# Part of w2 taken from the last load and brought in early by GpSimd, in a decode block on one Trainium2 core

## The chip, the cores and the metric

One core of a Trainium2 chip runs the whole program. The metric is the device time of one execution in microseconds; lower is better. The kernel before takes 1057.88 us (median of three runs, 1057.36 to 1058.01).

## What is computed

One token goes through a transformer block with conditioned layer norms. All arrays are fp32.

```
mod = (silu(c) @ w_mod).reshape(1, 6, 1, 640)      # sa, ca, ga, sb, cb, gb
h   = layernorm(x) * (1 + ca) + sa
x   = x + ga * attention(h, k_cache, v_cache, wq, wo)   # 32 heads, 8192 positions, 192 wide
h   = layernorm(x) * (1 + cb) + sb
x   = x + gb * (relu(h @ w1 + b1) ** 2 @ w2 + b2)       # 640 -> 1536 -> 640
```

The two caches are 403 MB together, each byte is used once, and all of it has to come from HBM.

## The kernel before

**Attention.** The loop over the 32 heads (L285) loads for each head the keys (`load_k`, one tile of 128 partitions by 64 positions by 192) and the values (`load_v`). A K tile carries, behind its keys, a slice of wq or wo that is needed soon. K, V and the large weights go round in three slots of one pool (`slot`, L54), so a load can be issued only when the tile that had its slot three allocations earlier has been read to the end. All of these loads are issued from SyncE's queue (SP), in program order; the instruction that issues one waits there for its slot.

`keys` (L192) multiplies the keys by the query on VectorE (L201), folds 7 of 16 positions in half on GpSimd (L203) and reduces on VectorE (L204, L205), in two pieces for a head and in four for the last one. `softmax` (L216) finds the maximum through a matmul with the identity (L220, L222) and takes the exponential on ScalarE (L228). `values` (L233) does 48 matmuls of p with V. `project` and `attend` carry the result of a pair of heads through wo. The order of every engine's instructions is the order in which the program is written (`manual_schedule`).

**Small columns.** `wm0`, the first load, ends with columns of x, c, b1 and b2 (L73); L76 copies them out. `spread` (L85) turns such columns into rows by a copy that repeats each value 32 times (L88) and a 32x32 transpose (L90); L284 makes `bbt`, the biases b1 and b2, before the first head.

**The tail.** After head 31 SyncE issues the rest of `wm1`, w1 in two pieces, gb, and w2 in five (L312 to L319). w2 comes last, since it is used last. Partition 32g+r holds the rows r, 32+r, ... of group g, where each of the four groups g has a quarter (384) of the 1536 hidden values; so w2 is 12 blocks b of 128 x 640, cut as 6, 3, 1, 1, 1 (`W2_CUT`). The compute of the tail is: `project(15)`, `attend(15)`, the residual and the second layer norm (L329 to L338), h @ w1 into four groups of 32 PSUM partitions, each 384 wide (`ps_f`, L343), bias, relu and square (`f`, L346 to L348), a transpose (`fT`, L349), the gate `gb` (L351), some matmuls into an unused bank (`ps_warm`, L355), then h @ w2 (`ps_y`, L363), 48 matmuls in order of b, and two VectorE instructions (L366, L367) before the output is stored (L368). A fp32 matmul of the program stands twice in the trace, as two passes.

Of the kernel before, what the change touches and what calls it, by code (L numbers as in the profile page):

```python
# [8 lines left out]
F32 = mybir.dt.float32  # L9
# [4 lines left out]
P = 128  # L14
D = 640
H = 32
# [3 lines left out]
G = 4  # L20
DG = D // G
FG = FF // G
KB = DG // 32
FB = FG // 32
PW = 2 * DH
E = 8
ED = 64
# [9 lines left out]
WITHOUT_W = (1, H - 2)  # L37
WITH_W = tuple(h for h in range(H) if h not in WITHOUT_W)
W1_CUT = ((0, 3), (3, 2))
W2_CUT = ((0, 6), (6, 3), (9, 1), (10, 1), (11, 1))  # L40
WARM = 2
EPS = 1e-5


@with_exitstack
def block_kernel(ctx: ExitStack, tc: tile.TileContext, kw, ky, vc, wm0, wm1, w1, gb, w2, out):
    nc = tc.nc
    const = ctx.enter_context(tc.tile_pool(name="const", bufs=1))
    strm = ctx.enter_context(tc.tile_pool(name="strm", bufs=3))
    work = ctx.enter_context(tc.tile_pool(name="work", bufs=2))  # L50
# [3 lines left out]
    def slot(name):  # L54
        return strm.tile([P, SLOT], F32, tag="slot", name=name, bufs=3)
# [16 lines left out]
    wm0_t = slot("wm0_t")  # L72
    nc.sync.dma_start(wm0_t[:, :wm0.shape[1]], wm0)  # L73

    small = const.tile([P, 2 * KB + FB + KB], F32, name="small")
    nc.vector.tensor_copy(small, wm0_t[:, KB * 2 * D + WQ:wm0.shape[1]])  # L76
    x_c, c_c, bbc = small[:, :KB], small[:, KB:2 * KB], small[:, 2 * KB:]

    def columns(src, n, name, pool=const, **how):

        t = pool.tile([P, n // 32, 32], F32, name=name, **how)
        nc.vector.transpose(t.rearrange("p b r -> p (b r)"), src)
        return t

    def spread(src, n, name):  # L85

        t = work.tile([P, FB + KB, 32], F32, name=name + "_c", tag="spread", bufs=1)
        nc.vector.tensor_copy(t[:, :n], src[:, :, None].to_broadcast([P, n, 32]))  # L88
        r = const.tile([P, 32 * n], F32, name=name)
        nc.vector.transpose(r, t[:, :n].rearrange("p b r -> p (b r)"))  # L90
        return r
# [38 lines left out]
    mods = const.tile([P, 6, DG], F32, name="mods")  # L130
# [19 lines left out]
    def load(src, to, h, what):  # L150
        to[h] = slot(f"{what}{h}")
        n, w = CUTS.get((what, h), 1), src.shape[1]
        for c in range(n):
            a, b = c * HD // n, (c + 1) * HD // n if c + 1 < n else w
            nc.sync.dma_start(to[h][:, a:b], src[:, a:b])

    def load_k(h):

        load(kw[WITH_W.index(h)] if h in WITH_W else ky[WITHOUT_W.index(h)], k_t, h, "k")

    def load_v(h):
        load(vc[h], v_t, h, "v")
# [14 lines left out]
    def query(i, w):  # L177
        w = w.rearrange("p (b n) -> p b n", b=KB)
        ps = psum.tile([P, 512], F32, tag="q", name=f"ps_q{i}", bufs=2)
        for b in range(KB):  # L180
            nc.tensor.matmul(ps[:, :PW], hR[:, b], w[:, b], start=(b == 0), stop=(b == KB - 1))  # L181
        qb_t[i] = work.tile([P, PW], F32, name=f"qb{i}", tag="qb")
        nc.scalar.activation(qb_t[i], ps[:, :PW], AF.Copy, scale=DH ** -0.5)  # L183
# [27 lines left out]
    def inverse(i):  # L211
        r = work.tile([P, 2], F32, tag="r", name=f"r{i}")
        nc.vector.reciprocal(r, sum_t.pop(i))
        ri_t[i] = r
# [30 lines left out]
    def project(i):  # L245

        n = 32 * NV
        os_ = work.tile([P, 2, ED], F32, tag="os", name=f"os{i}")
        inverse(i)
        r2 = ri_t.pop(i)  # L250
        for a in range(2):
            h = 2 * i + a
            om = work.tile([P, ED, E], F32, tag="om", name=f"om{h}", bufs=1)
            nc.vector.scalar_tensor_tensor(om[:n], ps_t.pop(h)[:n].rearrange("p (d e) -> p d e", e=E), r2[:n, a:a + 1],  # L254
                                           mask[:n, None, :].to_broadcast([n, ED, E]), op0=ALU.mult, op1=ALU.mult)
            nc.vector.tensor_reduce(os_[:n, a], om[:n], axis=AX.X, op=ALU.add)  # L256
        os_t[i] = psum.tile([P, 512], F32, tag="sm", name=f"ps_oT{i}", bufs=2)
        nc.tensor.matmul(os_t[i][:, :n], os_[:n].rearrange("p a d -> p (a d)"), quad[:n], start=True, stop=True)

    def attend(i, w):  # L260
        oT = work.tile([P, 96], F32, tag="oT", name=f"oT{i}")
        nc.vector.tensor_copy(oT, os_t.pop(i)[:, :96])  # L262
        w = w.rearrange("p (j n) -> p j n", j=3)
        if i + 1 < NPAIR:
            for j in range(3):
                for g in range(2):
                    nc.tensor.matmul(att_a[32 * g:32 * (g + 1), :2 * DG], oT[:, 32 * j:32 * (j + 1)],  # L267
                                     w[:, j, 2 * DG * g:2 * DG * (g + 1)], start=(i == 0 and j == 0), stop=(i == NPAIR - 2 and j == 2))
            return
        for j in range(3):  # L270
            for g in range(G):
                nc.tensor.matmul(att_t[0][32 * g:32 * (g + 1), :DG], oT[:, 32 * j:32 * (j + 1)],
                                 w[:, j, DG * g:DG * (g + 1)], start=False, stop=(j == 2))

    def gather():

        nc.scalar.activation(att_s[:64], att_a[:64, :2 * DG], AF.Copy)
        att_t.append(psum.tile([P, 512], F32, tag="o", name="att", bufs=3))
        for g in range(G):
            nc.tensor.matmul(att_t[0][32 * g:32 * (g + 1), :DG], ident[:, 32 * (g // 2):32 * (g // 2) + 1].to_broadcast([P, 32]),  # L280
                             att_s[:, DG * (g % 2):DG * (g % 2 + 1)], start=True, stop=False)

    x_t = spread(x_c, KB, "x_t")
    bbt = spread(bbc, FB + KB, "bbt")  # L284
    for h in range(H):  # L285
        i = h // 2
        if h:
            load_k(h)
        if h == H - 1:
            wm1_t = slot("wm1_t")  # L290
            nc.sync.dma_start(wm1_t[:, :WO + KB * D], wm1[:, :WO + KB * D])
        load_v(h)
        w = k_t[h][:, HD:]

        def between(c):
            if c == 0 and h % 2 and i:
                attend(i - 1, w)
            elif c == 0 and h % 2 == 0 and i + 1 < NPAIR:
                query(i + 1, w)
            elif c == 2 and h == H - 1:  # L300
                gather()

        if h % 2 and i:
            project(i - 1)
        sc = keys(h, between)
        p = softmax(h, sc)
        if h == H - 1:
            next(mod(2, 1, wm1_t[:, WO:WO + KB * D].rearrange("p (b n) -> p b n", b=KB)))
        values(h, p)
# [3 lines left out]
    w1_t = slot("w1_t")  # L313
# [3 lines left out]
    w2_t = slot("w2_t")  # L317
    for b0, n in W2_CUT:
        nc.sync.dma_start(w2_t[:, b0 * D:(b0 + n) * D], w2[:, b0 * D:(b0 + n) * D])  # L319
    gb_t = w1_t[:, KB * FF:KB * (FF + D)].rearrange("p (b n) -> p b n", b=KB)  # L320
    w1_t = w1_t[:, :KB * FF].rearrange("p (b n) -> p b n", b=KB)
    w2_t = w2_t[:, :FB * D].rearrange("p (b n) -> p b n", b=FB)

    project(NPAIR - 1)
    attend(NPAIR - 1, wm1_t[:, :WO])
    mod_b = mod(3, 2, wm1_t[:, WO + KB * D:WO + KB * 3 * D].rearrange("p (b n) -> p b n", b=KB), (2, 2, 1))
# [11 lines left out]
    hT2 = columns(layernorm(x1, 32, scale_b, lambda: mods[:, 3], "ln2", lambda: next(mod_b)), DG, "hT2")  # L338

    pf = psum.tile([P, 512], F32, tag="q", name="ps_f", bufs=2)  # L340
    for b in range(KB):
        for g in range(G):
            nc.tensor.matmul(pf[32 * g:32 * (g + 1), :FG], hT2[:, b], w1_t[:, b, FG * g:FG * (g + 1)],  # L343
                             start=(b == 0), stop=(b == KB - 1))
    f = work.tile([P, FG], F32, name="f", tag="spread", bufs=1)
    nc.vector.tensor_add(f, pf[:, :FG], bbt[:, :FG])  # L346
    nc.vector.tensor_scalar(f, f, 0.0, None, op0=ALU.max)
    nc.vector.tensor_mul(f, f, f)  # L348
    fT = columns(f, FG, "fT", work, tag="om", bufs=1)  # L349

    next(mod(5, 1, gb_t))  # L351
    idle = psum.tile([P, 512], F32, tag="sm", name="ps_warm", bufs=2)
# [1 line left out]
        for g in range(G):  # L354
            nc.tensor.matmul(idle[32 * g:32 * (g + 1)], ones[:, :32], w1_t[:, k, :512], start=True, stop=True)  # L355
    gb2 = const.tile([P, DG], F32, name="gb2")
    nc.vector.tensor_mul(gb2, mods[:, 5], bbt[:, FG:])
    nc.vector.tensor_add(x1, x1, gb2)

    py = psum.tile([P, 512], F32, tag="q", name="ps_y", bufs=2)  # L360
    for b in range(FB):
        for g in range(G):
            nc.tensor.matmul(py[32 * g:32 * (g + 1), :DG], fT[:, b], w2_t[:, b, DG * g:DG * (g + 1)],  # L363
                             start=(b == 0), stop=(b == FB - 1))
    y = const.tile([P, DG], F32, name="y")
    nc.vector.tensor_mul(y, py[:, :DG], mods[:, 5])  # L366
    nc.vector.tensor_add(y, y, x1)  # L367
# [43 lines left out]
```

## Time and profile before

| | |
|---|---|
| median of three runs | 1057.88 us |
| span of the profiled execution, from its first to its last instruction | 1055.5 us |
| busy in that span: TensorE, VectorE, GpSimd, ScalarE | 463.7, 831.4, 194.8, 33.4 us |
| read from HBM, mean rate | 451.82 MB, 428 GB/s |
| share of the 16 DMA engines that the load queue (q1) took | 99.3% |
| VectorE waiting for K tiles that carry a weight slice | 134.4 us |

The time of a run is 2.4 us more than the span of the profiled execution; what lies around the span isn't in the trace. The profile's page has one line for each engine's busy time, a picture of the span in 40 slices, the chain of work that ended last, and groups of instructions by line. The trace answers with waits (who waited for whom), with timelines of a stretch, and with busy times, granted TensorE clock and DMA share of a stretch. Line numbers (L201) are those of the kernel before.

### The profile page before, as it was taken

The page shows a single profiled execution, that of the slowest core. Times are in us where ns is not written, and L with a number is a line of the kernel's source. Part 1 is how long each engine was busy: PE and PEld are TensorE (multiplying, and loading weights), DVE is VectorE, ACT ScalarE, POOL GpSimd, SP SyncE. Part 2 cuts the span into 40 slices and gives each one's busy share as a digit, 9 for nine tenths or more (in the row PEclk, how much of TensorE's full clock was granted, in tenths as well). Part 3 has the DMA queues.
Part 4 walks back from the last instruction along what each step waited for, and adds up shares of the span by engine and source line. Part 5 has one row for each costly group of instructions (what it writes and reads, how often), then busy time and mean ns, then how long its engine had stood idle before and what let it go on. Part 6 is the DMA issues. An engine that isn't in the chain of part 4 may idle for free.

```text
span 1055.5 us, 5687 instructions
## 1 busy us (share of the span) xinstructions
PE 463.7 (44%) x2356; PEld 155.0 (15%) x2356; DVE 831.4 (79%) x409; ACT 33.4 (3%) x88; POOL 194.8 (18%) x72
## 2 busy tenths in 40 slices
PE   3234443355543345463334534335453335535446
PEld 1101111111111111120111111101111111111113
DVE  2886878978787987878888687997878798789963
ACT  1000000000000000000000000000000000000000
POOL 0211112211212221212221212221221221122110
PEclk9667666766666766666676666666666666767769
DMA  9999999999999999999999999999999999999997
GB/s 403 435 434 428 432 440 427 441 424 437 433 433 428 440 424 441 424 439 427 431 437 437 422 442 430 428 439 426 439 429 433 428 438 433 434 427 432 424 426 310
DMA packets 11410, 452.18 MB, mean 428 GB/s; under 512 B 1269, under 2 KB 1273, under 8 KB 1785
## 3 DMA queue, kind: packets, MB, share of 16 engines
q1 hardware_dynamic: 11384, 451.83, 99.3%
q8 instruction: 18, 0.29, 0.1%
q14 instruction: 8, 0.06, 0.0%
HBM read 451.82 MB, written 0.00 MB: 428 GB/s over the span
## 4 chain that ended last, share of the span: by engine, by line
DMA 42%; DVE 39%; PE 17%; ACT 1%; issue 1%; SPq 0%; DVEq 0%; ACTq 0%
DMA k<-in_kw 36%; DVE k L201 21%; PE ps_o L240 14%; DVE sc L204 12%; DVE sc L205 5%; DMA k<-in_ky 3%; DMA w_t<-in_w 2%; PE ps_mx L220 1%; DMA wm_t<-in_wm 1%; ACT p L228 1%; PE ps_sum L97 1%; PE ps_mod L140 1%; PE ps_q L181 1%; DVE nm L222 0%; DVE mp L218 0%
## 5 line engine op out<-in xcount | busy, mean ns | idle before, releaser
L201 DVE TENSOR_TENSOR k<-k,qb 128x6144 f32<-128x6144 f32 (+1 forms) x66 | 419.7, 6359 | 141.6 <-DMA k<-in_kw 134.4
L203 POOL TENSOR_TENSOR k<-k 128x1344 f32<-128x1344 f32 (+1 forms) x66 | 194.1, 2941 | 820.9 <-DVE k L201 476.1
L240 PE MATMUL ps_o<-v,p 128*32 128x512 f32 x1536 | 290.4, 731 | 17.2 <-ACT p L228 17.2
L204 DVE TENSOR_REDUCE sc<-k 128x18 f32<-128x3456 f32 (+1 forms) x66 | 240.5, 3644 | 4.3
L220 PE MATMUL ps_mx<-ident,mp 128*128 128x128 f32 x64 | 25.5, 501 | 416.2 <-DVE mp L218 416.2
L240 PEld LDWEIGHTS ps_o<-v,p 128*32 128x32 f32 x1536 | 68.4, 131 | 215.4 <-issue 193.1
L267 PE MATMUL att_a<-k,oT 128*32 128x320 f32 x180 | 49.6, 720 | 114.2 <-DVE oT L262 113.1
L205 DVE TENSOR_REDUCE sc<-k 128x14 f32<-128x1344 f32 (+1 forms) x66 | 99.0, 1500 | 0.0
L220 PEld LDWEIGHTS ps_mx<-ident,mp 128*128 128x128 f32 x64 | 16.1, 312 | 442.8 <-DVE mp L218 421.0
L181 PE MATMUL ps_q<-k,hR 128*128 128x384 f32 x150 | 52.3, 496 | 0.0
L228 ACT ACTIVATE p<-sc,nm 128x256 f32<-128x256 f32 x32 | 16.2, 508 | 760.6 <-DVE nm L222 496.9
L267 PEld LDWEIGHTS att_a<-k,oT 128*32 128x32 f32 x180 | 13.7, 161 | 136.7 <-DVE oT L262 116.7
L222 DVE TENSOR_REDUCE nm<-ps_mx 128x1 f32<-128x128 f32 x32 | 9.3, 291 | 28.5 <-PE ps_mx L220 28.5
L181 PEld LDWEIGHTS ps_q<-k,hR 128*128 128x128 f32 x150 | 27.3, 190 | 27.9 <-issue 11.7
L254 DVE SCALAR_TENSOR_TENSOR om<-ps_o,r,mask 96x512 f32<-96x512 f32 x32 | 23.9, 747 | 6.5 <-PE ps_o L240 5.4
L256 DVE TENSOR_REDUCE os<-om 96x64 f32<-96x512 f32 x32 | 21.8, 682 | 1.1
L140 PE MATMUL ps_mod<-wm_t,silu 128*32 128x320 f32 (+1 forms) x120 | 11.7, 550 | 14.6 <-DVE silu L128 14.6
L97 PE MATMUL ps_sum<-sp,ones 128*128 128x2 f32 x32 | 9.4, 364 | 17.2 <-ACT p L228 17.2
L183 ACT ACTIVATE qb<-ps_q 128x384 f32<-128x384 f32 x16 | 7.9, 491 | 195.2 <-PE ps_q L181 195.2
L97 PEld LDWEIGHTS ps_sum<-sp,ones 128*128 128x128 f32 x32 | 8.0, 312 | 21.9 <-ACT p L228 21.9
L145 DVE COPY mods<-ps_mod 128x320 f32<-128x320 f32 (+1 forms) x4 | 1.6, 398 | 10.2 <-PE ps_mod L140 10.2
L76 DVE COPY small<-wm_t 128x27 f32<-128x27 f32 x1 | 0.2, 179 | 11.2 <-DMA wm_t<-in_wm 11.2
(77 smaller groups left out, 90.9 us busy)
## 6 DMA issues: line engine op xcount, KB each, us to landing
k<-in_kw SPq DMA_DIRECT2D x29, 7104.0 KB, 27.4
v<-in_vc SPq DMA_DIRECT2D x32, 6144.0 KB, 22.1
k<-in_ky SPq DMA_DIRECT2D x1, 6144.0 KB, 28.3
k<-in_ky SPq DMA_DIRECT2D x2, 3072.0 KB, 21.5
k<-in_kw SPq DMA_DIRECT2D x3, 1536.0 KB, 15.5
wm_t<-in_wm SPq DMA_DIRECT2D x1, 4173.5 KB, 12.7
wm_t<-in_wm SPq DMA_DIRECT2D x1, 3200.0 KB, 29.3
wm_t<-in_wm SPq DMA_DIRECT2D x1, 2560.0 KB, 18.2
```

The lines of the kernel that those rows point to most:

```text
L97: nc.tensor.matmul(ps[:, :n], ones, src, start=True, stop=True)
L140: nc.tensor.matmul(ps[32 * g:32 * (g + 1), :n * DG], e[:, b:b + 1].to_broadcast([P, 32]), wb[:, :, DG * g:DG * (g + 1)], start=(b == 0), s ...
L181: nc.tensor.matmul(ps[:, :PW], hR[:, b], w[:, b], start=(b == 0), stop=(b == KB - 1))
L201: nc.vector.tensor_mul(pr, pr, q[:, None, :].to_broadcast([P, n, DH]))
L203: nc.gpsimd.tensor_add(half, half, pr[:, m:, DH // 2:])
L204: nc.vector.tensor_reduce(s[:, :m], pr[:, :m], axis=AX.X, op=ALU.add)
L205: nc.vector.tensor_reduce(s[:, m:], half, axis=AX.X, op=ALU.add)
L220: nc.tensor.matmul(ps[:, :P], mp.to_broadcast([P, P]), ident, start=True, stop=True)
L228: nc.scalar.activation(p, sc[:, :, None].to_broadcast([P, NPOS, 32 // E]), AF.Exp, bias=nm, accum_out=sp[:, h % 2:h % 2 + 1])
L240: nc.tensor.matmul(ps_t[h][32 * g:32 * (g + 1)], p[:, E * j:E * (j + 1)].rearrange("p e r -> p (e r)"), t[:, j, g], start=(j == 0), stop=( ...
L254: nc.vector.scalar_tensor_tensor(om[:n], ps_t.pop(h)[:n].rearrange("p (d e) -> p d e", e=E), r2[:n, a:a + 1], mask[:n, None, :].to_broadca ...
L267: nc.tensor.matmul(att_a[32 * g:32 * (g + 1), :2 * DG], oT[:, 32 * j:32 * (j + 1)], w[:, j, 2 * DG * g:2 * DG * (g + 1)], start=(i == 0 an ...
```

## The change

w2 is divided unevenly. The four groups now have 320, 320, 448 and 448 hidden values. The last load brings ten blocks for all 128 partitions (cut 5, 2, 1, 1, 1). Four more blocks, for partitions 64 to 127 alone, come from a new array `w2x` into a tile of their own, `w2x_t`. Behind them in each row of `w2x` stand 14 columns of b1 and 5 of b2, which leave `wm0`.

`w2x_t` is filled from GpSimd's queue in the iterations of heads 8, 10, ... 22. Each of these issues two transfers: the 19 bias columns (76 bytes a row) of eight rows of partitions 0 to 63, and eight rows of partitions 64 to 127 whole (2579 values, 10316 bytes a row). The eight rows are every fourth one of a group of 32. `bbt` is spread from `w2x_t`, 608 wide in place of 544, and this moves from before head 0 to the start of head 30's iteration, ahead of `keys(30)` on VectorE.

In the tail `ps_f` has groups 320 and 448 wide, `f` is 448 wide (a memset clears the part that partitions 0 to 63 don't have, and the bias is added in two instructions), and `ps_y` has 16 matmuls on partitions 64 to 127 with `w2x_t` ahead of 40 with w2.

```diff
-FB = FG // 32
+FB = 10
+FX = 4
+FT = FB + FX
+F0 = (0, 32 * FB, 64 * FB, 64 * FB + 32 * FT)
+FN = (32 * FB, 32 * FB, 32 * FT, 32 * FT)
+WX = FX * D + FT + KB
...
-W2_CUT = ((0, 6), (6, 3), (9, 1), (10, 1), (11, 1))
+W2_CUT = ((0, 5), (5, 2), (7, 1), (8, 1), (9, 1))
+X_AT = {8 + 2 * r: (r % 4) + 32 * (r // 4) for r in range(8)}
...
     x_t = spread(x_c, KB, "x_t")
-    bbt = spread(bbc, FB + KB, "bbt")
+    w2x_t = const.tile([P, WX], F32, name="w2x_t")
...
         load_v(h)
+        if h in X_AT:
+            r = X_AT[h]
+            top = 32 * (r // 32 + 1)
+            nc.gpsimd.dma_start(w2x_t[r:top:4, FX * D:], w2x[r:top:4, FX * D:])
+            nc.gpsimd.dma_start(w2x_t[64 + r:64 + top:4], w2x[64 + r:64 + top:4])
+        if h == H - 2:
+            bbt = spread(w2x_t[:, FX * D:], FT + KB, "bbt")
...
+    f = work.tile([P, 32 * FT], F32, name="f", tag="spread", bufs=1)
+    nc.vector.memset(f[:64, 32 * FB:], 0.0)
     project(NPAIR - 1)
...
-            nc.tensor.matmul(pf[32 * g:32 * (g + 1), :FG], hT2[:, b], w1_t[:, b, FG * g:FG * (g + 1)],
+            nc.tensor.matmul(pf[32 * g:32 * (g + 1), :FN[g]], hT2[:, b], w1_t[:, b, F0[g]:F0[g] + FN[g]],
                              start=(b == 0), stop=(b == KB - 1))
-    f = work.tile([P, FG], F32, name="f", tag="spread", bufs=1)
-    nc.vector.tensor_add(f, pf[:, :FG], bbt[:, :FG])
+    nc.vector.tensor_add(f[:, :32 * FB], pf[:, :32 * FB], bbt[:, :32 * FB])
+    nc.vector.tensor_add(f[64:, 32 * FB:], pf[64:, 32 * FB:32 * FT], bbt[64:, 32 * FB:32 * FT])
...
+    w2x_b = w2x_t[64:, :FX * D].rearrange("p (b n) -> p b n", b=FX)
+    for b in range(FX):
+        for g in range(G):
+            nc.tensor.matmul(py[32 * g:32 * (g + 1), :DG], fT[64:, FB + b], w2x_b[:, b, DG * g:DG * (g + 1)],
+                             start=(b == 0), stop=False)
     for b in range(FB):
         for g in range(G):
             nc.tensor.matmul(py[32 * g:32 * (g + 1), :DG], fT[:, b], w2_t[:, b, DG * g:DG * (g + 1)],
-                             start=(b == 0), stop=(b == FB - 1))
+                             start=False, stop=(b == FB - 1))
```

More of the change, by code (lines that the diff above doesn't have):

```diff
@@ L45, in block_kernel @@
 @with_exitstack
-def block_kernel(ctx: ExitStack, tc: tile.TileContext, kw, ky, vc, wm0, wm1, w1, gb, w2, out):
+def block_kernel(ctx: ExitStack, tc: tile.TileContext, kw, ky, vc, wm0, wm1, w1, gb, w2, w2x, out):
     nc = tc.nc
@@ L73, in block_kernel @@
     nc.sync.dma_start(wm0_t[:, :wm0.shape[1]], wm0)
-    small = const.tile([P, 2 * KB + FB + KB], F32, name="small")
+    small = const.tile([P, 2 * KB], F32, name="small")
     nc.vector.tensor_copy(small, wm0_t[:, KB * 2 * D + WQ:wm0.shape[1]])
-    x_c, c_c, bbc = small[:, :KB], small[:, KB:2 * KB], small[:, 2 * KB:]
+    x_c, c_c = small[:, :KB], small[:, KB:2 * KB]
     def columns(src, n, name, pool=const, **how):
@@ L85, in spread @@
     def spread(src, n, name):
-        t = work.tile([P, FB + KB, 32], F32, name=name + "_c", tag="spread", bufs=1)
+        t = work.tile([P, FT + KB, 32], F32, name=name + "_c", tag="spread", bufs=1)
         nc.vector.tensor_copy(t[:, :n], src[:, :, None].to_broadcast([P, n, 32]))
@@ L342, in block_kernel @@
         for g in range(G):
-            nc.tensor.matmul(pf[32 * g:32 * (g + 1), :FG], hT2[:, b], w1_t[:, b, FG * g:FG * (g + 1)],
+            nc.tensor.matmul(pf[32 * g:32 * (g + 1), :FN[g]], hT2[:, b], w1_t[:, b, F0[g]:F0[g] + FN[g]],
                              start=(b == 0), stop=(b == KB - 1))
-    f = work.tile([P, FG], F32, name="f", tag="spread", bufs=1)
-    nc.vector.tensor_add(f, pf[:, :FG], bbt[:, :FG])
+    nc.vector.tensor_add(f[:, :32 * FB], pf[:, :32 * FB], bbt[:, :32 * FB])
+    nc.vector.tensor_add(f[64:, 32 * FB:], pf[64:, 32 * FB:32 * FT], bbt[64:, 32 * FB:32 * FT])
     nc.vector.tensor_scalar(f, f, 0.0, None, op0=ALU.max)
     nc.vector.tensor_mul(f, f, f)
-    fT = columns(f, FG, "fT", work, tag="om", bufs=1)
+    fT = columns(f, 32 * FT, "fT", work, tag="om", bufs=1)
     next(mod(5, 1, gb_t))
@@ L356, in block_kernel @@
     gb2 = const.tile([P, DG], F32, name="gb2")
-    nc.vector.tensor_mul(gb2, mods[:, 5], bbt[:, FG:])
+    nc.vector.tensor_mul(gb2, mods[:, 5], bbt[:, 32 * FT:])
     nc.vector.tensor_add(x1, x1, gb2)
     py = psum.tile([P, 512], F32, tag="q", name="ps_y", bufs=2)
+    w2x_b = w2x_t[64:, :FX * D].rearrange("p (b n) -> p b n", b=FX)
[3 more added lines that the diff above has]
+                             start=(b == 0), stop=False)
     for b in range(FB):
@@ L385, in column, with hidden @@
         return a(v).reshape(G, n, 32).transpose(0, 2, 1).reshape(P, n)
+    def hidden(v):
+        b = np.zeros((P, FT), np.float32)
+        for g in range(G):
+            b[32 * g:32 * (g + 1), :FN[g] // 32] = a(v)[F0[g]:F0[g] + FN[g]].reshape(-1, 32).T
+        return b
+    w2 = a(B_w2)
+    w2m = np.stack([w2[F0[g]:F0[g] + 32 * FB].reshape(FB, 32, D).transpose(1, 0, 2) for g in range(G)])
+    w2e = np.stack([w2[F0[g] + 32 * FB:F0[g] + 32 * FT].reshape(FX, 32, D).transpose(1, 0, 2) for g in (2, 3)])
     wq = a(A_wq).reshape(G, KB, 32, NPAIR, PW).transpose(3, 0, 2, 1, 4).reshape(NPAIR, P, WQ)
@@ L396 @@
         "vc": a(A_v_cache).reshape(H, P, NPOS // E, E, NV, ED).transpose(0, 1, 2, 4, 5, 3).reshape(H, P, HD),
-        "wm0": np.concatenate([rows(wm[:, :2 * D], KB), wq[0], column(A_x, KB), column(c, KB),
-                               column(B_b1, FB), column(B_b2, KB)], axis=1),
+        "wm0": np.concatenate([rows(wm[:, :2 * D], KB), wq[0], column(A_x, KB), column(c, KB)], axis=1),
         "wm1": np.concatenate([wo[-1], rows(wm[:, 2 * D:3 * D], KB), rows(wm[:, 3 * D:5 * D], KB)], axis=1),
@@ L401 @@
         "gb": rows(wm[:, 5 * D:], KB),
-        "w2": rows(B_w2, FB),
+        "w2": np.ascontiguousarray(w2m.reshape(P, FB * D)),
+        "w2x": np.concatenate([np.concatenate([np.zeros((64, FX * D), np.float32), w2e.reshape(64, FX * D)]),
+                               hidden(B_b1), column(B_b2, KB)], axis=1),
     }
```

## The prediction, made before the change was run

> **What bounds the kernel now.** I read the page first (span, the DMA row, the chain), then the chain of waits over the last 150 us piece by piece, then VectorE's timeline there, and last the DMA share stretch by stretch. From the page, and from the view that divides the span into stretches (columns: length, busy time and count of each engine, granted TensorE clock, DMA share, GB/s):
>
> ```profile
> span 1055.5 us, 5687 instructions
> q1 hardware_dynamic: 11384, 451.83, 99.3%
> q8 instruction: 18, 0.29, 0.1%
> ```
> ```profile
> 31.00:939.00 908.00, 392.71 (x1784) 125.76 (x1785) 738.05 (x315) 26.57 (x75) 175.52 (x58) 0.68 1.00 433
> ```
>
> Until 939 us the 16 DMA engines are full, at 433 GB/s, which is 27.1 GB/s for each engine. In that stretch every byte added to the queue delays what is behind it. The question is what happens after 939. Two pieces of the chain that ended last (start, length, what):
>
> ```profile
> 912.48 26.83 DMA k<-in_kw
> 939.31 0.03 issue
> 939.34 0.02 DVEq L201
> 939.36 0.04 issue
> 939.40 6.57 DVE k L201
> ...
> 964.30 0.06 DVE nm L222
> 964.36 0.14 issue
> 964.50 6.56 DVE k L201
> ```
> ```profile
> 1032.07 19.60 DMA w_t<-in_w
> 1051.67 0.04 issue
> 1051.71 0.52 PE ps_y L363 x8
> ```
>
> and VectorE's timeline, where the bracket is the idle time before an instruction:
>
> ```profile
> 939.40 6.56 DVE L201 TENSOR_TENSOR k<-k,qb 128x6144 f32<-128x6144 f32 x1 [3.24 <-DMA k<-in_kw]
> 964.50 6.55 DVE L201 TENSOR_TENSOR k<-k,qb 128x6144 f32<-128x6144 f32 x1
> 999.05 0.26 DVE L262 COPY oT<-ps_oT 128x96 f32<-128x96 f32 x1 [0.38 <-PE ps_oT L258]
> 1030.28 0.74 DVE L254 SCALAR_TENSOR_TENSOR om<-ps_o,r,mask 96x512 f32<-96x512 f32 x1 [5.37 <-PE ps_o L240]
> ```
>
> Head 29's keys land at 939.31, and this is VectorE's last wait for a transfer. From there heads 29, 30 and 31 run one behind the other: VectorE, the maximum through TensorE, the exponential, 48 matmuls, `project`, the layer norm, `ps_f`, `f`, `ps_y`. No step of it before `ps_y` waits for data from HBM. So two strands meet at `ps_y`: a compute strand that hangs on 939.31, and the transfers of w2, which end at 1051.67. Today the transfers end last. How much later?
>
> ```profile
> 1044.38 1.57 PE L140 MATMUL ps_mod<-w_t,silu 128*32 128x160 f32 x40
> 1047.46 3.16 PE L363 MATMUL ps_y<-w_t,fT 128*32 128x160 f32 x80
> 1050.92 0.48 PE L363 MATMUL ps_y<-w_t,fT 128*32 128x160 f32 x8 [0.31 <-DMA w_t<-in_w]
> 1051.71 0.48 PE L363 MATMUL ps_y<-w_t,fT 128*32 128x160 f32 x8 [0.31 <-DMA w_t<-in_w]
> ```
>
> The gate's matmuls (L140) have the same shape and wait for nothing: 40 in 1.57, 0.039 us each. At that pace the 96 of `ps_y` would take 3.77 and end at 1051.2, where in the trace they end at 1052.2. So the compute strand has only **1.0 us of room**. That is the number to watch: anything over 1.0 us that is put on the compute strand lengthens the kernel.
>
> **The change, part by part.**
>
> *Fewer bytes at the end.* Two blocks less of w2 for all partitions: 2 x 128 x 2560 bytes = 655 KB, at 433 GB/s 1.5 us less on the last transfers. Worth at most 1.0 us, after which the compute strand ends last; and it is worth nothing if that strand grows.
>
> *The same bytes earlier.* Heads 8 to 22 lie in the stretch where DMA is full, so the 8 x 8 x 10316 = 660 KB delay all later tiles, head 29's keys among them. Spread over all 16 engines that is 660 KB / 433 = 1.5 us. But each transfer has eight rows. If eight engines take one row each and always the same eight, each of them gets 82.5 KB more, at 27.1 GB/s **3.05 us**, and a tile is complete when its slowest engine is. What matters then is whether those eight have room. At the end of the span the queue runs dry and shows this:
>
> ```profile
> 1047.00:1048.00 1.00, 1.00 (x25) 0.70 (x20) 0.67 (x3) 0.00 (x0) 0.00 (x0) 1.00 0.60 241
> 1048.00:1049.00 1.00, 1.00 (x39) 0.98 (x31) 0.00 (x0) 0.00 (x0) 0.00 (x0) 1.00 0.58 221
> 1049.00:1050.00 1.00, 0.98 (x31) 0.66 (x24) 0.00 (x0) 0.00 (x0) 0.00 (x0) 1.00 0.54 197
> 1050.00:1051.00 1.00, 0.69 (x24) 0.27 (x19) 0.00 (x0) 0.00 (x0) 0.00 (x0) 1.00 0.15 59
> ```
>
> A DMA share of 0.58 is nine engines of 16 at work: about seven are through shortly after 1047, nine only after 1049.5, and the last at 1051.67. So the engines do drift apart, by 3 to 4 us over the run. Seven are early, yet eight get the extra rows: whichever eight they are, at least one of the late nine is among them. That one ends 0 to 1.5 us ahead of the last, and so with 3.05 us more it ends 1.5 to 3.05 us after it. I take the middle: **head 29's keys 2.3 us late**. That the same engines are late by about as much at 939 as at the end is an estimate; the views don't name an engine. Below, 0 would be right if the drift had a different pattern there; above, a foreign packet on an engine may cost more than its bytes. The nearest row is q8, the instruction fetches: 0.1% of 16 x 1055.5 us over 18 packets is 0.94 us for 16 KB, where 27.1 GB/s gives 0.6; by that ratio 3.05 becomes 4.7 us, and that is the upper end.
>
> [...]
>
> *`bbt` spread at head 30.* The trace has both instructions, 544 wide:
>
> ```profile
> L88 DVE COPY bbt_c<-small x1: 720/720/720, 25.6 to 25.6; 128x544 f32<-128x544 f32 x1
> L90 DVE STREAM_TRANSPOSE bbt<-bbt_c x1: 746/746/746, 26.4 to 26.4; 128x544 f32<-128x544 f32 x1
> ```
> ```profile
> 31.56 6.56 DVE L201 TENSOR_TENSOR k<-k,qb 128x6144 f32<-128x6144 f32 x1 [4.44 <-ACT qb L183]
> ```
>
> Where they stood they cost nothing: VectorE idled 4.44 us behind them, until ScalarE delivered the first query, and that is gone with no gain. Their new place is 964.50, between two instructions with no gap: 1.466 x 608/544 = **1.64 us** on the compute strand. Queued behind them is everything from head 30 on, and SyncE's loads of head 31, w1 and w2 with it; these have enough transfers ahead of them to stay fed.
>
> *GpSimd.* Sixteen issues, each pair ahead of the fold of its head. GpSimd idles 16.5 us before such a fold (POOL L203 at 914.85, next fence), so some microseconds of issuing are hidden. If they took over 16, VectorE's L205 would be late. I cost them at nothing.
>
> ```profile
> 914.85 3.03 POOL L203 TENSOR_TENSOR k<-k 128x1344 f32<-128x1344 f32 x1 [16.48 <-DVE k L201]
> ```
>
> *The tail's compute.* From the groups of instructions by line (busy, mean ns) between 1039 and 1053:
>
> ```profile
> L343 PE MATMUL ps_f<-w_t,hT 128*32 128x384 f32 x40 | 5.1, 680 | 2.1 <-issue 2.1
> L355 PE MATMUL ps_warm<-w_t,ones 128*32 128x512 f32 x16 | 1.9, 592 | 0.0
> ```
>
> The four groups of a set run side by side. A set 512 wide takes 1.9/4 = 0.48 us, a set 160 wide 1.57/10 = 0.16, so 64 columns more are worth 0.06. If the widest group rules, ten sets of `ps_f` cost 0.6 us more; if the mean width rules, which stays 384, nothing; by the 5.1 us as traced, 17% or 0.85. I take **0.6**. `ps_y` grows from 48 to 56 matmuls, 16 records of 0.039: **0.63**. The memset falls into VectorE's 5.37 us wait at 1030. The rest of `f`:
>
> ```profile
> 1046.23 0.58 DVE L82 STREAM_TRANSPOSE fT<-f 128x384 f32<-128x384 f32 x1
> ```
>
> `fT` is done at 1046.81 and `ps_y` starts at 1047.46, behind the gate and `ps_warm`. One instruction more (about 0.3) and 17% on three others (0.25) just fill that 0.65. Without that cover they would cost up to 0.5.
>
> The clock is a spread of its own:
>
> ```profile
> 1040.00:1046.00 6.00, 6.00 (x80) 3.41 (x76) 1.28 (x3) 0.00 (x0) 0.00 (x0) 0.72 0.99 413
> ```
>
> During `ps_f` it was granted 0.72. Before, this was hidden by w2's arrival; on a strand that ends last it counts. [...] I put 0.8 us to either end of the range for it, from the 5.1 us at 0.72 against full clock (1.4 us).
>
> **Sum.** Compute strand: 2.3 + 1.64 + 0.6 + 0.63 = 5.17, less the 1.0 of room: +4.2 us. The transfers end 1.5 us later at worst (3.05 less 1.5), so the compute strand ends last. The profiled span 1055.5 becomes 1059.7; the median of the runs stands 2.4 above the span, so 1057.88 becomes **1062.0**.
>
> **The rivals.**
> 1. *A foreign packet costs more than its bytes.* For it: the q8 row. Against it: that row is rounded to one digit. Then 4.7 in place of 2.3: 1064.4.
> 2. *The extra rows find room* and head 29's keys land at 939.3 as before. For it: seven engines that end over 2 us early. Against it: eight don't fit on seven. Then 1.87 is left: 1059.7, which is no difference that counts (0.2%, 2.1 us, is about what a measurement of this kernel can tell from none).
> 3. *Faster.* The place is head 30's start: if its keys came later than 966.1 (964.50 + 1.64), `bbt` would fit into a wait, and with the eight engines ending early the transfers of w2 would still decide; 1.5 us less of them gives 1056.4. It decides from compute additions under 1.0 us. Against it: VectorE went from 964.30 to 964.50 without a wait.
> 4. *The rows don't go to a fixed half*, but round all engines: 1.5 in place of 2.3, 1061.2; slower still.
>
> **How the numbers follow.** Forecast 0.62, rival 1 0.17, rival 2 0.13, rival 3 0.05, rival 4 0.03. Slower 0.82, same 0.13, faster 0.05. The range runs from rival 2 less some of the clock's spread, 1059.2, to rival 1 with 0.25 more for `ps_f` and the clock's 0.8, 1065.5.
>
> **What would show it.** VectorE's last wait for keys should end near 941.6 in place of 939.4. At head 30 a copy and a transpose 608 wide should take 1.6 us with no idle time around them. `ps_y` should run through without a wait for w2, and the chain that ended last should go from L201 to the end through VectorE and TensorE with no transfer behind 942. It would be wrong if a transfer still ended the chain, or if head 29's keys came no later.

## The result, and the profile after

The changed kernel takes 1068.56 us (median of four runs, 1067.17 to 1069.47) where the kernel before takes 1057.66 (four runs, 1057.36 to 1058.01). The ratio is 1.0103, with a 95% interval of 1.0091 to 1.0114: 10.9 us slower, in the direction of the forecast (1062.0) and beyond its range (1059.2 to 1065.5). The profiled executions differ by 9.4 us in span; the other 1.5 us is the spread of the executions and what lies around the span.

The page of the changed kernel shows hardly less traffic and one new queue:

```profile
span 1064.9 us, 5747 instructions
q1 hardware_dynamic: 11384, 451.16, 98.9%
q0 software_dynamic: 512, 0.67, 0.2%
```

q0 is GpSimd's queue: 0.67 MB, 0.2% of the engines' time. By bytes it is nothing. The view by stretches tells more. For 31 to 249 us, and for 249 to 755 us, in which the sixteen transfers lie, first before and then after (next to last column the DMA share, last column GB/s, all queues together):

```profile
31.00:249.00 218.00, 88.80 (x401) 28.70 (x402) 177.39 (x74) 7.94 (x20) 42.38 (x14) 0.68 1.00 433
249.00:755.00 506.00, 223.79 (x1038) 71.25 (x1029) 411.48 (x177) 13.55 (x40) 96.83 (x32) 0.68 1.00 433
```
```profile
31.00:249.00 218.00, 88.72 (x409) 28.89 (x410) 177.01 (x74) 7.45 (x19) 42.36 (x14) 0.67 1.00 432
249.00:755.00 506.00, 215.15 (x984) 69.46 (x978) 405.79 (x174) 13.53 (x40) 104.88 (x48) 0.67 1.00 427
```

Up to 249 us hardly anything is lost. From there the DMA share is 1.00 as before, but the engines move 427 GB/s in place of 433. Six of 433 over 506 us is some 7 us, and since the new bytes are counted in the 427, their own 1.5 us come on top. The engines weren't waiting: packets took longer. The trace's records of single packets say so directly. The stream's large packets have 49152 or 56832 bytes and usually take about 1821 or 2101 ns. From 249 to 755 us 241 of 4064 took over a tenth longer (before, 13 of 4131), and what all of them together took above these two times adds up to 6.4 us for each of the 16 engines (0.3 before). VectorE's timeline has the consequence:

```profile
948.29 6.56 DVE L207 TENSOR_TENSOR k<-k,qb 128x6144 f32<-128x6144 f32 x1 [3.25 <-DMA k<-in_kw]
960.25 6.55 DVE L207 TENSOR_TENSOR k<-k,qb 128x6144 f32<-128x6144 f32 x1
973.55 0.79 DVE L94 COPY bbt_c<-w2x_t 128x608 f32<-128x608 f32 x1
974.38 0.81 DVE L96 STREAM_TRANSPOSE bbt<-bbt_c 128x608 f32<-128x608 f32 x1
975.11 6.52 DVE L207 TENSOR_TENSOR k<-k,qb 128x6144 f32<-128x6144 f32 x1
```

Head 29 starts at 948.29 in place of 939.40: 8.9 us, where 2.3 were forecast. `bbt` takes 1.6 us without idle time, as forecast. The chain of waits ends as forecast too: behind head 29's keys no transfer stands in it.

```profile
920.77 27.43 DMA k<-in_kw
948.29 6.57 DVE k L207
...
1050.44 2.99 PE ps_f L358 x31
...
1055.76 1.72 PE ps_warm L370 x14
1057.48 1.22 PE ps_y L379 x32
1058.70 2.90 PE ps_y L383 x80
1061.62 0.33 DVE y L386
```

### The profile page after: what moved, and what is told of

Read it like the earlier page. It is cut to its first block, busy times and chain, and to the rows that moved or that the text cites. A ratio compares the mean times of both kernels' runs of the same rounds, so it can differ in the third digit from the quotient of the medians.

```text
span 1064.9 us, 5747 instructions
## 1 busy us (share of the span) xinstructions
PE 460.6 (43%) x2372; PEld 155.0 (15%) x2372; DVE 832.1 (78%) x411; ACT 33.4 (3%) x88; POOL 202.8 (19%) x88
## 4 chain that ended last, share of the span: by engine, by line
DMA 41%; DVE 39%; PE 18%; issue 1%; ACT 1%; DVEq 0%; ACTq 0%
DMA k<-in_kw 36%; DVE k L207 21%; PE ps_o L246 13%; DVE sc L210 12%; DVE sc L211 5%; DMA k<-in_ky 3%; PE ps_mx L226 1%; DMA wm_t<-in_wm 1%; PE ps_mod L146 1%; ACT p L234 1%; PE ps_sum L103 1%; PE ps_q L187 0%; DVE nm L228 0%; DVE mp L224 0%; PE ps_f L358 0%
```

## The experiments

Head 29's start on VectorE is the measure for the stream. In the kernels with the new tail the compute strand ends last, so that the time follows head 29 less the 1.0 us of room; in the kernel before with something added the last transfer of w2 still ends the chain, and the room doesn't count. Every comparison is with runs of the kernel before on the same chip (medians 1057.76, 1057.87 and 1057.66 us in the three groups). Where "the kernel before plus" transfers is run, their data are never read.

### Four kernels on which part of the transfers costs the time

Three theories stood at the start: a fixed price for each GpSimd transfer (A), a price of the large rows whatever issues them (B), a price of the 76-byte rows (C).

**sp_queue**, the changed kernel with both transfers issued by SyncE:

```diff
-            nc.gpsimd.dma_start(w2x_t[r:top:4, FX * D:], w2x[r:top:4, FX * D:])
-            nc.gpsimd.dma_start(w2x_t[64 + r:64 + top:4], w2x[64 + r:64 + top:4])
+            nc.sync.dma_start(w2x_t[r:top:4, FX * D:], w2x[r:top:4, FX * D:])
+            nc.sync.dma_start(w2x_t[64 + r:64 + top:4], w2x[64 + r:64 + top:4])
```

> The changed kernel with its sixteen early transfers issued from SyncE's queue in place of GpSimd's, at the same places. Theory A (each transfer from GpSimd's queue costs all 16 engines about 0.4 us beyond its bytes, (8.0 - 1.5) / 16): only the bytes stay, head 29's keys come 1.5 to 3.1 us later than before (941 to 942.5), and the kernel is 2 to 3.7 us above before. Rival B (the large rows cost the extra, whatever the queue) and rival C (the 76-byte rows cost it, whatever the queue): head 29 starts near 948.3 and the time stays near 1068.

Measured: 1067.71 us, ratio 1.0096 (1.0083 to 1.0109).

```profile
948.23 6.56 DVE L207 TENSOR_TENSOR k<-k,qb 128x6144 f32<-128x6144 f32 x1 [3.24 <-DMA k<-in_kw]
```

Head 29 is as late as with GpSimd (948.29). Neither the queue nor GpSimd's work of issuing is the cause; A falls as a price of GpSimd's queue.

**no_tiny**, the changed kernel without the tiny transfers (the bias columns come with `wm0` again, `bbt` is spread before head 0):

```diff
-            nc.gpsimd.dma_start(w2x_t[r:top:4, FX * D:], w2x[r:top:4, FX * D:])
-            nc.gpsimd.dma_start(w2x_t[64 + r:64 + top:4], w2x[64 + r:64 + top:4])
+            nc.gpsimd.dma_start(w2x_t[64 + r:64 + top:4, :FX * D], w2x[64 + r:64 + top:4, :FX * D])
```

> The changed kernel without the eight transfers of 76-byte rows: the bias columns come with the first load as before, and bbt is spread before head 0. Theory A: eight transfers in place of sixteen, so 1.5 + 8 x 0.4 = 4.7 us at head 29 (944.1), and with bbt's 1.64 gone the kernel is about 3.5 us above before. Rival B (large rows, 0.8 each): 8.0 us at head 29 (947.4), 6.9 above before. Rival C (76-byte rows, 0.8 each): 1.5 us at head 29 (940.9), 0.4 above before.

Measured: 1062.68 us, ratio 1.0068 (1.0039 to 1.0096), with a wide scatter (1061.09 to 1074.07). In its profile head 29 starts at 948.31, as late as with the tiny rows, but that is no proof for B: the execution took 1066.97, and from 271 to 316 us its stream lost 4.6 us in one piece, which no other profile shows and which stays unexplained. Of the eight large transfers the seven later ones each cost the stream 0.4 to 0.7 us by the excess of its packets; in the changed kernel each costs 0.6 to 0.9. So the large rows are dear without the tiny ones, but how much of the delay is theirs has to be read from rows_hi, below. The time says little too, since the stream buffers lie elsewhere in this kernel, which turned out to matter (pad, below).

**tiny_only**, the kernel before plus the tiny transfers:

```diff
+    probe_t = const.tile([P, 19], F32, name="probe_t")
...
+        if h in X_AT:
+            r = X_AT[h]
+            top = 32 * (r // 32 + 1)
+            nc.gpsimd.dma_start(probe_t[r:top:4], wm1[r:top:4, :19])
```

> The kernel before with nothing but eight transfers of eight 76-byte rows from GpSimd added, at heads 8 to 22, into a tile that nothing reads: 4.9 KB in all. Theory A: 8 x 0.4 = 3.2 us at head 29 (942.6) and 3.2 us on the whole, since w2's transfers are late by as much. Rival B: no difference from before. Rival C: 6.5 us at head 29 and on the whole.

Measured: 1054.96 us, ratio 0.9975 (0.9964 to 0.9985). C falls; and that eight added transfers make the kernel 2.8 us faster was expected by no theory. In the records of single packets the gain is there from the first head on, long before the first tiny transfer.

**one_each**, the changed kernel with one transfer of 64 large rows and one of tiny rows for all partitions, both at head 8:

```diff
-        if h in X_AT:
...
+        if h == 8:
+            nc.gpsimd.dma_start(w2x_t[:, FX * D:], w2x[:, FX * D:])
+            nc.gpsimd.dma_start(w2x_t[64:, :FX * D], w2x[64:, :FX * D])
```

> The changed kernel with the early bytes in two GpSimd transfers at head 8, one of 64 whole rows and one of 128 rows of 76 bytes, in place of sixteen of eight rows. Theory A: two transfers, 1.5 + 0.8 = 2.3 us at head 29 (941.7), 2.8 above before. Rival B (same number of large rows, so the same cost): 8 us at head 29, about 8.5 above before. Rival C (twice as many 76-byte rows as now): more than 8 us.

Measured: 1065.69 us, ratio 1.0076 (1.0063 to 1.0089). By stretches of 5 us, around the transfer:

```profile
275.00:280.00 5.00, 5.00 (x28) 1.27 (x31) 0.00 (x0) 0.00 (x0) 0.00 (x0) 0.69 1.03 338
280.00:285.00 5.00, 5.00 (x32) 1.76 (x27) 2.24 (x1) 0.00 (x0) 0.00 (x0) 1.00 1.09 301
285.00:290.00 5.00, 2.02 (x7) 0.87 (x5) 4.90 (x2) 0.49 (x1) 0.45 (x1) 1.00 0.92 297
```

For 15 us the core gets about 310 GB/s in place of 433, with all engines busy; 655 KB at 433 GB/s would have taken 1.5 us. Head 29 is 6.6 us late, where sixteen transfers made it 8.9. So most of the delay is there without the many transfers: it is the rows.

### What about the rows, and what made tiny_only faster

Two theories for the rows: their place, so that what they cost the stream hangs on which partitions the rows of a transfer go to (the expectations call it the theory of the ports), or that any row on only some of the engines throws the sixteen streams out of step (the theory of the step). Which places would be cheap no trace had shown; it was the author's guess. What a dear place costs was taken from the changed kernel, 7 to 9 us at head 29, and a cheap one from the bytes. If the place decides, rows_hi was expected at 1065 to 1067 us, rows_lo at 1059.3 to 1061, all_parts at 1059.3 to 1062 and rows_block at 1065 to 1068; if the step decides, rows_hi and rows_lo both at 1065 to 1067 and all_parts at 1059.3 to 1062. And one theory for tiny_only: its unused tile of 76 bytes moves everything allocated behind it.

**pad**, the kernel before plus an unused tile:

```diff
+    pad_t = const.tile([P, 24], F32, name="pad_t")
+    nc.vector.memset(pad_t, 0.0)
```

> The kernel before with one unused tile of 96 bytes per partition among the constants (written once with zeros, never read) and nothing else; it moves the three large stream buffers from byte 35488 to byte 35584 of each partition, that is from 32 past a multiple of 128 to a multiple of 128. The run tiny_only had the same shift beside its tiny transfers and was 2.8 us faster than before. Theory of the address: the gain is the buffers' place, so this kernel gains the same, about 1055.0 us, with head 29's keys about 2 us earlier and every 49152-byte packet at 1815 ns from the first head on. Rival: the tiny transfers gave the gain, then this kernel is at 1057.8 us, with the packets' mix of 1815, 1818 and 1825 ns as before.

Measured: 1055.06 us, ratio 0.9973 (0.9963 to 0.9983): the gain of tiny_only without any transfer.

```profile
937.27 6.56 DVE L201 TENSOR_TENSOR k<-k,qb 128x6144 f32<-128x6144 f32 x1 [3.12 <-DMA k<-in_kw]
```

Head 29 starts at 937.27 in place of 939.40. From the packet records, between 85 and 245 us, the 49152-byte packets (640 in each). Where the slots start is added up from the tiles allocated ahead of them:

```
kernel     slots start at byte   past a multiple of 256   mean ns   at most 1816 ns
before     35488                 160                      1821.6    42%
after      46016                 192                      1822.1    18%
tiny_only  35584                 0                        1817.5    97%
pad        35584                 0                        1816.7    98%
all_three  46080                 0                        1817.6    97%
```

That is 0.27% on these packets; the 56832-byte ones have 2101.7 against 2098.8 ns, 0.14%. On a stream of 940 us that makes 1.3 to 2.5 us, and head 29 is 2.1 us earlier. That the place of the slots is the reason is shown by pad; why, is not, and a multiple of 128 is not told apart from one of 256.

**rows_hi**, the kernel before plus the eight transfers of large rows, from another tensor:

```diff
+    probe_t = const.tile([P, 4 * D], F32, name="probe_t")
...
+        if h in X_AT:
+            r = X_AT[h]
+            top = 32 * (r // 32 + 1)
+            nc.gpsimd.dma_start(probe_t[64 + r:64 + top:4], wm1[64 + r:64 + top:4, :4 * D])
```

> The kernel before plus, at heads 8 to 22, the eight large transfers alone: eight rows of 10240 bytes for partitions 64 to 127, taken from another tensor of HBM than in the changed kernel, into a tile that nobody reads; w2 stays as it was, and the stream buffers keep their place against a multiple of 512 bytes. The bytes alone are 1.5 us. [...] Theory of the source (the new tensor's place in HBM collides with the stream's): 1.5 us, about 1059.3.

**rows_lo**, the same to the lower half:

```diff
-            nc.gpsimd.dma_start(probe_t[64 + r:64 + top:4], wm1[64 + r:64 + top:4, :4 * D])
+            nc.gpsimd.dma_start(probe_t[r:top:4], wm1[r:top:4, :4 * D])
```

> As rows_hi, but the same rows go to partitions 0 to 63. [...] Theory of the step: the same as rows_hi, 1065 to 1067 us. Theory of the source: 1059.3 as in rows_hi.

**all_parts**, as many transfers and bytes, each to all partitions:

```diff
+        if h in X_AT:
+            c = (h - 8) // 2 * (D // 4)
+            nc.gpsimd.dma_start(probe_t[:, c:c + D // 4], wm1[:, c:c + D // 4])
```

> As rows_hi, with the same number of transfers, the same bytes in each, at the same heads and from the same queue, but each goes to all 128 partitions, 640 bytes for each. [...] If any second transfer in the full stream costs what was measured, it is 1065 to 1067 as well, and the shape of the rows isn't the cause.

**rows_block**, as rows_lo with eight neighbouring partitions for each transfer:

```diff
-            r = X_AT[h]
-            top = 32 * (r // 32 + 1)
-            nc.gpsimd.dma_start(probe_t[r:top:4], wm1[r:top:4, :4 * D])
+            r = 4 * (h - 8)
+            nc.gpsimd.dma_start(probe_t[r:r + 8], wm1[r:r + 8, :4 * D])
```

> As rows_lo (the kernel before plus eight transfers of eight rows of 10240 bytes, never read), but the eight rows of a transfer go to eight neighbouring partitions (0 to 7, then 8 to 15, to 56 to 63) and not to every fourth one. [...] Rival: only the upper half of the partitions is dear, for whatever reason, and this costs what rows_lo costs, 1059.6 us.

Measured: rows_hi 1065.54 us, ratio 1.0073 (1.0061 to 1.0086); rows_lo 1059.64, 1.0017 (1.0008 to 1.0026); all_parts 1059.92, 1.0019 (1.0010 to 1.0028); rows_block 1068.30, 1.0100 (1.0086 to 1.0114). The stretch of the transfers, in this order of kernels (last column GB/s):

```profile
249.00:755.00 506.00, 216.22 (x990) 69.47 (x987) 406.63 (x174) 13.54 (x40) 100.80 (x40) 0.68 1.00 427
```
```profile
249.00:755.00 506.00, 224.87 (x1017) 71.46 (x1014) 408.95 (x177) 13.54 (x40) 100.81 (x40) 0.68 1.00 432
```
```profile
249.00:755.00 506.00, 224.05 (x1017) 71.49 (x1014) 409.58 (x177) 13.53 (x40) 100.85 (x40) 0.68 1.00 433
```
```profile
249.00:755.00 506.00, 215.77 (x990) 69.44 (x984) 404.71 (x170) 12.94 (x38) 100.86 (x40) 0.68 1.00 426
```

and VectorE's timeline at head 29, in the same order:

```profile
947.81 6.56 DVE L202 TENSOR_TENSOR k<-k,qb 128x6144 f32<-128x6144 f32 x1 [3.25 <-DMA k<-in_kw]
```
```profile
941.99 6.56 DVE L202 TENSOR_TENSOR k<-k,qb 128x6144 f32<-128x6144 f32 x1 [3.24 <-DMA k<-in_kw]
```
```profile
941.45 6.56 DVE L202 TENSOR_TENSOR k<-k,qb 128x6144 f32<-128x6144 f32 x1 [3.25 <-DMA k<-in_kw]
```
```profile
950.51 6.56 DVE L202 TENSOR_TENSOR k<-k,qb 128x6144 f32<-128x6144 f32 x1 [3.23 <-DMA k<-in_kw]
```

The same 655 KB, in as many transfers, from the same queue and tensor, cost head 29 8.4, 2.6, 2.0 and 11.1 us. rows_lo and rows_block even read the same 64 rows of `wm1` and write the same 64 partitions; they differ only in which eight go together. The lower half is cheap with every fourth partition and the dearest of all with neighbours, so neither "the upper half" nor "any row on some engines" is the reason; one_each says the same of the latter, since by the packet records its 64 rows are spread over all 16 engines. The source falls as well: rows_hi reads `wm1` and the changed kernel `w2x`, at much the same cost. What is left is where the rows of one transfer go. Two of the kernels differ in what they read together too (rows_hi has rows 64 to 127 of `wm1`, and each transfer of rows_block has eight neighbouring rows of it); this wasn't tried apart.

The single large rows show it (packet records, 64 in each kernel; 10240 bytes at 27.1 GB/s would be 378 ns):

```
kernel      min / median / max ns
rows_lo     385 / 388 / 394
rows_hi     386 / 512 / 640
rows_block  385 / 425 / 1121
```

But they are not where the time goes: rows_block has the lower median and the greater delay. It goes into the stream's own packets beside them. For 249 to 755 us, with the number of the 49152- and 56832-byte packets that took over a tenth longer than 1821 and 2101 ns, and what all these packets together took above the two times, for each of the 16 engines:

```
kernel      long packets   excess, us   head 29 later, us
rows_block  162            7.2          11.1
changed     241            6.4           8.9
sp_queue    201            6.3           8.8
rows_hi     171            5.9           8.4
one_each     77            3.9           6.6
mirror       18            0.5           2.7
rows_lo      15            0.3           2.6
all_parts    13            0.4           2.0
before       13            0.3           0
```

(mirror follows below.) The order is that of the delays, up to the last two, and what the cheap kernels are late by is about the bytes, 1.5 to 3.05 us.

The trace names no engine, and no run shows what the stream's packets meet beside such rows. So why the one place is cheap and the other dear is open; that the place decides is shown, from 2.0 to 11.1 us at head 29.

### The changed kernel without each cause

**mirror**, the further blocks on partitions 0 to 63 and the tiny rows on 64 to 127:

```diff
-F0 = (0, 32 * FB, 64 * FB, 64 * FB + 32 * FT)
-FN = (32 * FB, 32 * FB, 32 * FT, 32 * FT)
+F0 = (0, 32 * FT, 64 * FT, 64 * FT + 32 * FB)
+FN = (32 * FT, 32 * FT, 32 * FB, 32 * FB)
...
-            nc.gpsimd.dma_start(w2x_t[64 + r:64 + top:4], w2x[64 + r:64 + top:4])
+            nc.gpsimd.dma_start(w2x_t[r:top:4], w2x[r:top:4])
```

> The changed kernel turned round: the four further blocks of w2 lie on partitions 0 to 63 and the tiny rows with bias columns go to partitions 64 to 127; the same bytes, the same number of transfers, the same work for every engine. Theory of the ports: the difference of rows_hi and rows_lo, 5.9 us, is saved, 1068.6 - 5.9 = 1062.7 us, and head 29's keys come at about 942.5. Rival (the cost hangs on the pairing of tiny and large rows, or on what the rest of the changed kernel does to the stream): 1067 to 1069 us as the changed kernel.

Measured: 1062.37 us, ratio 1.0043 (1.0030 to 1.0055).

```profile
942.12 6.56 DVE L207 TENSOR_TENSOR k<-k,qb 128x6144 f32<-128x6144 f32 x1 [3.25 <-DMA k<-in_kw]
```

Its 64 large rows take 388 to 394 ns, those of the changed kernel 388 to 479. Turning the layout round takes 6.2 us off head 29's delay, with not a byte less; 5.9 of them are the excess of the stream's packets (6.4 against 0.5 in the table).

**bias_early**, the changed kernel with the spreading moved:

```diff
-        if h == H - 2:
+        if h == 24:
             bbt = spread(w2x_t[:, FX * D:], FT + KB, "bbt")
```

> The changed kernel with the spreading of the bias columns (the 608 wide copy and transposition) ahead of head 24 in place of head 30. There VectorE waits for the stream, and the 1.6 us lie in that wait. The prediction's term: from head 29 on the compute strand sets the end, so 1.6 us are saved, 1068.6 - 1.6 = 1067.0 us, and head 30 is later than before by what head 29 is later. Rival: the 1.6 us were absorbed further on, 1068.6 us.

Measured: 1066.00 us, ratio 1.0078 (1.0065 to 1.0092).

```profile
948.63 6.56 DVE L207 TENSOR_TENSOR k<-k,qb 128x6144 f32<-128x6144 f32 x1 [3.24 <-DMA k<-in_kw]
960.59 6.55 DVE L207 TENSOR_TENSOR k<-k,qb 128x6144 f32<-128x6144 f32 x1
973.73 6.55 DVE L207 TENSOR_TENSOR k<-k,qb 128x6144 f32<-128x6144 f32 x1
```

From head 29 to head 30 it is 25.10 us, as before (964.50 - 939.40), where the changed kernel has 26.82. So 1.72 us are taken off the compute strand. The medians differ by 2.6 from the changed kernel's; with intervals this wide that agrees with 1.7, and isn't a size of its own.

**all_three**, both edits and an unused tile of 16 floats ahead of the slots:

```diff
     w2x_t = const.tile([P, WX], F32, name="w2x_t")
+    pad_t = const.tile([P, 16], F32, name="pad_t")
+    nc.vector.memset(pad_t, 0.0)
```

> The changed kernel with three edits together: mirrored as in mirror, bias columns spread ahead of head 24 as in bias_early, and an unused tile of 64 bytes that puts the stream buffers at a multiple of 512 bytes. If the three causes are separate and add up: 1068.6 - 5.9 - 1.6 - 2.7 = 1058.4 us, the last term from pad against before, since the packets of the changed kernel show the same mix of 1815, 1818 and 1825 ns as before's. If they share a cause, it stays above 1060. Either way it is not expected below pad's 1055.1, since the bytes of the rows (about 1.8 us by rows_lo) are in the stream ahead of head 29's keys.

Measured: 1058.09 us, ratio 1.0004 (0.9995 to 1.0013), as the kernel before, and slower than pad.

```profile
939.94 6.56 DVE L207 TENSOR_TENSOR k<-k,qb 128x6144 f32<-128x6144 f32 x1 [3.18 <-DMA k<-in_kw]
```

The three savings add up (1058.4 was expected), though the slots' place is no part of what the change cost: the kernel before has them off a multiple of 256 as well. With all three the changed kernel is still about 3 us behind the kernel that has only the pad. The fastest kernel is pad, with tiny_only, which has the same shift, beside it.

## Why the prediction was wrong

Its frame held (head 29's keys come later, the compute strand ends last, 1.0 us of room), and one term was far too small, because what makes a foreign row dear wasn't in it. The terms, in the profiled executions:

| term | forecast | measured |
|---|---|---|
| head 29's keys | 2.3 | 8.9 |
| `bbt` on the strand, head 29 to head 31 | 1.64 | 1.7 |
| head 31 to the start of `ps_y` | 0.6 | -0.6 |
| `ps_y`, above 3.77 | 0.63 | 0.4 |
| room | -1.0 | -1.0 |
| sum | 4.2 | 9.4 |

**The step that failed** is "each of them gets 82.5 KB more, at 27.1 GB/s 3.05 us", with "whichever eight they are" behind it: the rows were priced by their bytes on the engine that carries them, as if it were the same where they go. Which partitions they go to decides. Where the rows go to a cheap place the step is right: mirror has head 29 2.7 us late and rows_lo 2.6, both inside its 1.5 to 3.05. In the changed kernel 6.2 us come on top. (That mirror's time is 1062.4 where 1062.0 was forecast is in part luck, see the tail.) The loss isn't that of eight engines, either. In the packet records one packet starts where another ends, so that they can be followed as 16 streams. At each of the eight transfers in the changed kernel and in rows_hi eight streams carry a row (at two of these sixteen only seven could be followed), and all 16 lose time on their own packets, 0.45 us at least and 0.64 to 0.91 in the mean, those without a row somewhat more than those with one. In rows_lo and mirror a stream loses 0.01 us as a rule. In the changed kernel the eight means add up to 6.0 us, nearly the whole of the 6.2. Head 29's keys show it at the end: by their completion events the first of the 16 engines is through at 943.38 (935.71 before) and the last at 948.20 (939.31); VectorE starts on the keys 0.09 us after the last, in both kernels.

**Rival 1** ("a foreign packet on an engine may cost more than its bytes") came nearest, and took its price from the instruction fetches, 4.7 us at the upper end. Its mechanism isn't the right one either: the foreign rows themselves took 404 ns in the median, where their bytes alone at 27.1 GB/s make 381; it is the stream's packets beside them that grew. The fetches' row was no bound, because those packets say nothing of where in the memory a row goes. So the range ended at 1065.5, below the result. With no row in the trace for such a transfer, the range needed a wider end.

**Always the same eight engines**, one row each, was an assumption in the 3.05 us, and no run shows this term, since the trace names no engine. What the runs showed in its place are 2.6 us (rows_lo), 2.7 (mirror) and 8.9 (the changed kernel) at head 29. The first two lie within 1.5 to 3.05. In rows_lo and rows_hi transfers of eight follow one another with nothing between. No row of rows_lo is slow (394 ns at most), and rows_hi falls behind rows_lo at each of its eight transfers, by 0.5 to 0.9 us at the starts of the heads, so that one transfer costs about what the next does. In rows_lo the 16 engines also drift apart as they would if the same eight took a row each time: between the first and the last completion event of a tile lie 2.4 us at 263 us and 6.2 at 754, in all_parts, whose transfers go to all 128 partitions, 2.4 and 4.1.

**GpSimd at nothing** was right: an issue takes 0.5 to 0.7 us in the view by tile (min/median/max in ns), and sp_queue, in which GpSimd issues none, is as slow.

```profile
L302 POOL DMA_DIRECT2D w2x_t<-in_w2x x8: 541/542/679, 270.0 to 717.6; - x8
L303 POOL DMA_DIRECT2D w2x_t<-in_w2x x8: 518/518/524, 270.7 to 718.1; - x8
```

**The tail.** `ps_f` was to cost 0.6 more, and took less (groups by line; 5.1, 680 before):

```profile
L358 PE MATMUL ps_f<-w_t,hT 128*32 128x320 f32 (+1 forms) x40 | 4.0, 488 | 2.1 <-issue 2.1
```

The granted clock was 1.00 in that stretch where it had been 0.72, and this outweighs the wider group. What the width alone costs can be read from rows_hi and pad, which have `ps_f` 384 wide and were granted 1.00 there: 3.4 us, 488 ns. So the width cost the forecast 0.6 us (4.0 less 3.4: the widest group rules), and the clock gave back 1.7 (5.1 less 3.4), where the prediction put 1.4 for the whole of it and 0.8 at either end of its range. The term as a whole goes with the clock: from head 31 to `ps_f` it was 47.0 to 47.5 us in the nine profiles with a mean granted clock of 0.81 there, and 47.9 to 49.5 in the five with 0.76 or 0.77 (bias_early, sp_queue, rows_block, mirror, all_three). So mirror, with the same tail, has +1.0 where the changed kernel has -0.6. `ps_y` ran from 1057.41 to 1061.6 without a wait. The last transfer of w2 landed at 1059.38, 7.7 us later than before and not 1.5; it still came ahead of its use, since the compute strand had moved by more.

**Not asked at all** was where the slots lie. The change moves them from 35488 to 46016, both off a multiple of 256, and the 49152-byte packets took 1821.6 and 1822.1 ns. So it cost nothing here, but only by chance.

## What to carry to other kernels

In this stream, with a DMA share of 1.00, a small transfer for part of the partitions was priced by where its rows go, not by its bytes alone: the same 655 KB made head 29 2.6 to 11.1 us late by the choice of partitions, and 2.0 when spread over all 128. So try the mirrored layout, or all partitions, before dropping such an idea. When an experiment adds a tile, check where the buffers behind it come to lie: 96 unused bytes were worth 2.8 us, more than the 1.0 us that this change could have brought. And when a cost has no neighbouring row in the trace, the range's end has to be set by what it could block, and the nearest row of another kind is no bound.

## What the runs showed of the hardware that was not expected

- Rows in a dear place slowed all sixteen engines, not only the eight that carried them: at each transfer of the changed kernel every one of the 16 streams lost 0.57 us or more on its own packets, at a DMA share of 1. Why the others lose time too was not shown.
- Transfers of 128 rows of 640 bytes (all_parts, 2.0 us) cost no more than ones of eight rows of 10240 bytes in a cheap place (rows_lo, 2.6 us), with sixteen times as many rows. The trace has 256 packets for them, of 640 and 4480 bytes, where it has 64 for the others.
- Eight transfers of eight 76-byte rows cost nothing that can be measured: 0.9975 (0.9964 to 0.9985) with them, 0.9973 (0.9963 to 0.9983) without, both with the slots at byte 35584.
